# An attention and mixture-of-experts kernel: loads and TensorE order planned anew, with a charge for DMA issues that meet an instruction fetch

## The chip, the cores and the metric

One core of a Trainium2 chip runs the whole program. The metric is the device time of one execution in microseconds (us). TensorE is PE in the profile, its weight loads PEld, VectorE DVE, ScalarE ACT, GpSimd POOL, and SyncE, which issues every DMA of this kernel, SP.

## The reference, cut to what matters

```
scores = (q @ k.T) / 8                     # 8 batches, 8 heads, 576 tokens, 64 per head, float32
mask   = heads 0-3: the last 32 tokens; heads 4-7: every 32nd token
x      = softmax(scores + mask) @ v        # heads side by side: x is (8, 576, 512)
w      = softmax over the two largest of x @ w_gate, for 4 experts
out    = sum over chosen experts e:  w_e * (causal_softmax(x wq_e (x wk_e).T / 8) @ (x wv_e)) @ wo_e
```

## The kernel before, in words

The kernel is a list of 517 operations for TensorE and many more for the other engines, made batch by batch, and a planner (`schedule`, from line 584) that runs a small cost model of the chip at build time and emits every instruction in the order that it finds. At run time each engine executes its own list strictly in that order and waits on semaphores.

**Stage 1** of a batch works on four pairs of heads, called h0 to h3 here; h0 and h1 are local, h2 and h3 strided. For each pair q and k are loaded into a `nat` tile: a local pair by four issues (line 868, 144 KB each), a strided one by two loads of three issues (line 875). `tp` transposes it on PE in two halves u0 and u1 (line 921), copies bring the result to SBUF, `s` makes the scores (line 954), mask and softmax follow on DVE, POOL and ACT, and `xa` multiplies with v (line 1047 local, 1066 strided). The v of a local pair is two loads of four issues (line 898), of a strided pair one load of six (line 906). There are two buffers for `nat` and two for v (`VR`); the local pairs of batch 0 use other buffers for `nat`. So the q and k of a pair can be loaded only when `tp` of the last but one pair has ended, and its v when an earlier `xa` has ended.

**Stage 2** projects x with three-term split float32: `pj` makes q and k (line 1197; line 1208 in batch 0, there in parts of three matmuls, one for each pair of heads), `vp` and `vp4` the values and the gate (lines 1144 and 1128), `s2` and `s2_4` the causal scores (lines 1282 and 1262), `t2` transposes the probabilities (line 1336), `acc` multiplies with the values (line 1369) and `yp` with wo (line 1398); then the result is stored (lines 1407 to 1410). The weights come in at the start by line 814 (with line 817 for the gate) and are split into a high and a low half (lines 820 and 823).

**What sets the order.** `PRI` (line 109) holds a number for each operation, by kind and batch. For a PE operation the whole part is its turn: PE takes turn 0, 1, 2 and so on to 516, whatever is ready. For any other operation the number is added to a key that the program gives; among the operations of an engine that can start at the same time the planner takes the lowest key. For the loads that key, from batch 1 on, is `k0 - 30` for q and k and `k0 - 25` for v, with `k0 = 52 * (batch + 0.25 * pair)`; for batch 0 it is the pair (v: 4 + the pair), and for the weights 6.5, 7.5 and 12.5 for wk, wq and wv plus 0.1 for each slice. A load takes a free buffer when it is issued. The planner also models the fetch of PE's instructions in blocks of 256:

```
if x == ask:
    coming, ask = at + FETCH, ask + 256
else:
    end += max(here - at, 0.0)
    here, part = coming, part + 256
```

and an issue on SP as a fixed time `ask_`, a share of the DMA engines' time, and a wait for one of eight lanes (from line 674).

Of the kernel before, what the change touches and what calls it, by code (L numbers as in the profile page):

```python
# [20 lines left out]
def attention_moe_kernel(  # L21
# [59 lines left out]
    class Ring:  # L81
# [16 lines left out]
        def take(self, buf):  # L98
# [485 lines left out]
    FETCH, DMALAT = 4.2, 1.7  # L584
# [891 lines left out]
```

## Time and profile before

| | us |
|---|---|
| median of 3 runs | 464.77 (463.95 to 467.97) |
| time of the profiled execution | 465.67 |
| its span, first to last instruction | 463.9 |
| PE busy | 442.1 (95%) |
| DVE, ACT, POOL busy | 334.7, 280.3, 214.6 |

The profiled execution's time is 1.77 us more than its span, and 0.9 us above the median. The kernel's bytes are 41.94 MB of DMA at a mean of 90 GB/s. A reader should look at PE's idle time first, then at the clock that was granted while it ran, and then at which stretch of the span either falls into.

### The profile page before, as it was taken

What the parts mean: (1) busy time and instruction counts of PE and PEld (TensorE: products, weight loads), DVE (VectorE), ACT (ScalarE), POOL (GpSimd) and SP (SyncE); (2) the same over time, 40 slices, a digit from 0 to 9 for tenths busy, and PEclk for the clock granted to TensorE, in tenths of its full rate; (3) what the DMA queues carried; (4) which work ended last, traced back from release to release, by engine and by line L of the source; (5) the groups of instructions that cost most, each with busy time, mean ns of one, the idle gap of its engine ahead of it and who ended that gap; (6) DMA issues with size and microseconds to landing.
All of it is one profiled execution on the core that took longest, in us unless ns stands there. A gap on an engine that the chain in (4) does not pass through costs nothing.

```text
span 463.9 us, 19970 instructions
## 1 busy us (share of the span) xinstructions
PE 442.1 (95%) x8198; PEld 396.7 (86%) x8198; DVE 334.7 (72%) x1096; ACT 280.3 (60%) x846; POOL 214.6 (46%) x384
## 2 busy tenths in 40 slices
PE   6599897989999999999999999999999999999996
PEld 5598795879989998899988899899988998899874
DVE  3867766886766879967798874786689866746760
ACT  3356666854675659746497364766567537826552
POOL 5474277546234616823447425352446624250440
PEclk9659987999999999999999999999999999999999
DMA  8556634454144027383156601534034302200013
GB/s 138 128 138 139 156 98 105 116 139 94 30 128 107 11 65 149 108 130 83 39 137 162 106 28 53 152 79 101 27 76 152 86 1 58 68 23 4 24 69 114
DMA packets 82619, 41.94 MB, mean 90 GB/s; under 512 B 70752, under 2 KB 74208, under 8 KB 82528
## 3 DMA queue, kind: packets, MB, share of 16 engines
q1 hardware_dynamic: 82528, 40.66, 36.3%
q8 instruction: 65, 1.06, 1.0%
q14 instruction: 26, 0.21, 0.2%
HBM read 31.20 MB, written 9.44 MB: 88 GB/s over the span
## 4 chain that ended last, share of the span: by engine, by line
PE 85%; SPq 6%; DMA 4%; issue 2%; ACT 1%; DVE 1%; POOL 0%; ACTq 0%
PE bank L1197 20%; PE bank L1398 11%; PE bank L1144 10%; PE bank L1369 10%; PE bank L1282 7%; PE bank L1336 6%; PE bank L954 5%; PE bank L921 4%; PE bank L1047 3%; PE bank L1262 3%; PE bank L1066 2%; SPq L868 2%; DMA nat<-in_k_dram 2%; SPq L898 2%; PE bank L1128 2%
## 5 line engine op out<-in xcount | busy, mean ns | idle before, releaser
L1317 POOL TENSOR_SCALAR p<-p,st,wt 128x384 f32<-128x384 f32 (+3 forms) x128 | 76.5, 616 | 62.2 <-DVE st L1301 31.5
L1294 ACT ACTIVATE p<-p,st 128x256 f32<-128x256 f32 (+3 forms) x128 | 71.8, 567 | 1.5 <-DVE st L1289 1.1
L1289 DVE CUSTOM_DVE_ANT_0 p<-bank,m_cau 128x384 f32<-128x384 f32 (+3 forms) x128 | 56.5, 485 | 3.1 <-PE bank L1282 2.0
L1217 ACT CAST qk<-bank 128x288 fp32r<-128x288 f32 x64 | 25.6, 400 | 52.1 <-PE bank L1197 51.6
L1369 PE MATMUL bank<-th,vs 128*64 128x192 f32 (+4 forms) x512 | 49.8, 343 | 0.0
L1219 DVE TENSOR_TENSOR qkl<-bank,qk 128x288 fp32r<-128x288 f32 x64 | 28.5, 451 | 26.1 <-ACT qk L1217 25.9
L729 ACT COPY qkt<-bank 128x324 f32<-128x324 f32 (+2 forms) x90 | 35.0, 429 | 19.7 <-PE bank L921 19.3
L729 ACT COPY th<-bank 128x384 f32<-128x384 f32 (+2 forms) x107 | 43.0, 433 | 5.4 <-PE bank L1336 4.6
L1369 PEld LDWEIGHTS bank<-th,vs 128*64 128x64 f32 x512 | 34.2, 139 | 13.5 <-issue 6.9
L1336 PE MATMUL bank<-ident,p 64*128 64x64 f32 x800 | 39.8, 227 | 0.3 <-DVE ol L1382 0.3
L1032 DVE TENSOR_TENSOR xl<-bank,xh 128x160 fp32r<-128x160 f32 (+4 forms) x112 | 30.6, 327 | 12.9 <-ACT xh L1030 11.6
L1336 PEld LDWEIGHTS bank<-ident,p 64*128 64x128 f32 x800 | 33.5, 140 | 6.5 <-issue 2.6
L921 PE MATMUL bank<-ident,nat 54*128 54x54 f32 (+1 forms) x636 | 31.9, 236 | 7.4 <-DMA nat<-in_q_dram 2.4
L1144 PE MATMUL bank<-wh_v,xh 128*128 128x260 f32 x128 | 36.6, 286 | 0.0
L1144 PE MATMUL bank<-wh_v,xl 128*128 128x260 f32 x128 | 36.3, 283 | 0.0
L1144 PE MATMUL bank<-wl_v,xh 128*128 128x260 f32 x128 | 36.0, 281 | 0.0
L1030 ACT CAST xh<-bank 128x160 fp32r<-128x160 f32 (+4 forms) x112 | 27.0, 320 | 14.6 <-PE bank L1047 10.1
L954 PE MATMUL bank<-qkt 64*32 64x64 f32 (+1 forms) x2048 | 32.7, 233 | 3.3 <-issue 2.4
L921 PEld LDWEIGHTS bank<-ident,nat 54*128 54x128 f32 (+1 forms) x636 | 27.1, 148 | 10.1 <-DMA nat<-in_q_dram 2.6
L989 POOL TENSOR_TENSOR p1l<-p1l,st 128x640 f32<-128x640 f32 (+1 forms) x18 | 20.5, 1143 | 29.3 <-DVE st L987 23.9
L954 PEld LDWEIGHTS bank<-qkt 64*32 64x32 f32 (+1 forms) x2048 | 28.5, 122 | 6.0 <-issue 3.5
L729 ACT COPY ys<-bank 128x512 f32<-128x512 f32 x29 | 17.0, 586 | 27.4 <-PE bank L1398 24.5
(154 smaller groups left out, 1336.5 us busy)
## 6 DMA issues: line engine op xcount, KB each, us to landing
out_dram<-ys SPq DMA_DIRECT2D x32, 256.0 KB
nat<-in_q_dram SPq DMA_DIRECT2D x28, 144.0 KB
nat<-in_k_dram SPq DMA_DIRECT2D x28, 144.0 KB
nat<-in_k_dram SPq DMA_DIRECT2D x32, 99.0 KB
nat<-in_q_dram SPq DMA_DIRECT2D x32, 99.0 KB
v<-in_v_dram SPq DMA_DIRECT2D x64, 48.0 KB
v<-in_v_dram SPq DMA_DIRECT2D x48, 54.0 KB
nat<-in_k_dram SPq DMA_DIRECT2D x16, 90.0 KB
```

Source lines behind the costliest of these rows:

```text
L729: (nc.scalar.copy if e == "ACT" else nc.vector.tensor_copy)(dst, src)
L921: nc.tensor.transpose(tp[x].t[:, w_ * (g - g0):w_ * (g - g0) + w_], blk, ident[r, r])
L954: nc.tensor.matmul(o, lhs, rhs, start=True, stop=True)
L1144: nc.tensor.matmul(vp.t[:m, :NV], xx.t[:, t0:t0 + m], ww.t[:, kt, :], start=i == 0, stop=i == 11)
L1197: nc.tensor.matmul(pj.t[:, :HS], ww.t[:, kt, ep * 128:(ep + 1) * 128], xx.t[:, c], start=i == 0, stop=i == 11)
L1282: nc.tensor.matmul(sp[a].t[:, :nk], x.t[r, 0, q0:q0 + 128], y.t[r, 1, :nk], start=i == 0, stop=i == 2)
L1289: lambda e, sp=sp, p=p, a=a, nk=nk, ci=ci: nc.vector.tensor_tensor_reduce(out=p.t[:, a, :nk], in0=sp[a].t[:, :nk], in1=m_cau[:, S - nk:], ...
L1294: op("exp2", {"ACT": 0.33 + 0.00083 * nk}, k_ + 1, lambda e, p=p, a=a, ci=ci, nk=nk: nc.scalar.activation(p.t[:, a, :nk], p.t[:, a, :nk], ...
L1317: lambda e, p=p, a=a, ci=ci, t=t, nk=nk: nc.gpsimd.tensor_scalar(p.t[:, a, :nk], p.t[:, a, :nk], st.t[:, 14 + ci + a:15 + ci + a], wt.t[:, ...
L1336: nc.tensor.transpose(tp[hf].t[:, 64 * c:64 * c + 64], src, ident[r, r])
L1369: nc.tensor.matmul(acc.t[o, c0:c0 + cn], vw, th[a].t[:, s0:s0 + cn], start=j == 0, stop=j == idx[-1], skip_group_check=True)
L1398: nc.tensor.matmul(yp.t[:, :DM], xx.t[:, c0:c0 + 128], ww.t[:, ep, :], start=i == 0, stop=i == 5)
```

## The change

The planner gets one more rule: when an instruction fetch has been asked for (0.5 us after the asking point), the next DMA issue on SP that lies close to that moment takes 1.0 us longer. All numbers in `PRI` are new, 517 of them turns of PE: 120 operations keep their turn, 229 move by one or two, and the farthest moves by 40. Nothing else differs: the same instructions on the same engines, the same buffers, the same data.

```
     PRI = {
...
-        "load_qk 1": [-54.5, -39.5, -359, -18.5, -36, -5.5, -29.5, 18.5, -39, -10, 37, -25],
-        "load_qk 2": [-17.5, 30, -29.5, -12, 23, 37, -26.5, 3.5, 7.5, -32, -54, -15.5],
+        "load_qk 1": [-203.5, -40.5, -578, -55.5, -242, 12.5, -49.5, -47, -35.5, -210, 58.5, -123.5],
+        "load_qk 2": [36, -5.5, -109.5, 8.5, 18.5, -36, 18.5, -44, 9, -33.5, -69.5, 25.5],
...
-        "load_v 1": [41.5, -14.5, 55, 2, 18, 18],
-        "load_v 2": [9, 17.5, 4.5, 4, -72, 8],
+        "load_v 1": [176.5, -19, -10.5, 340.5, 12.5, 34.5],
+        "load_v 2": [94.5, 36.5, 37.5, 160.5, 52.5, 90.5],
...
-        "load_w 0": [-277.5, -154, -57.5, -48, -227, -231, -55, -99, -5, -3, -5.5, -15, 478, 491],
+        "load_w 0": [-254.5, -220, -214.5, -77.5, -282.5, -245.5, -160, -59.5, -26, -30.5, -50, -34.5, 375,
+            562],
...
-        "pj 0": [18, 23, 33, 36, 21, 30, 32, 35, 19, 25, 27, 38, 16.01, 22, 28, 34, 17, 24, 31, 37, 53, 59, 63,
-            67, 58, 60, 62, 65, 57, 61, 66, 68],
+        "pj 0": [24, 29, 35, 36, 17, 20, 26, 34, 15.01, 22, 31, 38, 19, 23, 30, 33, 16, 28, 32, 37, 55, 61, 64,
+            68, 51, 54, 60, 66, 59, 62, 65, 67],
...
-        "tp 0": [3.02, 4, 1.02, 2, 8, 7.02, 10.02, 11],
-        "tp 1": [40, 39.01, 54.02, 56, 69, 55.04, 75.04, 82],
-        "tp 2": [81.02, 85, 97, 95.02, 106.04, 107, 100.03, 105],
+        "tp 0": [4, 3.02, 2, 1.02, 8, 7.02, 10.02, 12],
+        "tp 1": [39.01, 40, 56.02, 58, 69, 57.03, 74.04, 83],
+        "tp 2": [85, 81.02, 93.02, 94, 107, 104.04, 101, 98.04],
...
-        "vp 0": [50, 49, 51, 52],
+        "vp 0": [50, 53, 49, 47.01],
...
-        "vp4 0": [47.01],
+        "vp4 0": [52],
...
-        "xa 0": [12.01, 15.01, 20.04, 29.03],
-        "xa 1": [64.03, 88.03, 101.04, 110.04],
+        "xa 0": [11.02, 14.01, 21.03, 27.03],
+        "xa 1": [63.03, 89, 109, 110.02],
...
-        "yp 0": [139, 137, 103, 134],
+        "yp 0": [132, 136, 102, 174],
...
-    FETCH, DMALAT = 4.2, 1.7
+    FETCH, DMALAT, STEAL = 4.2, 1.7, 1.0
...
+        asked = 0.0
...
-                        coming, ask = at + FETCH, ask + 256
+                        coming, ask, asked = at + FETCH, ask + 256, at + 0.5
...
                     x = max(x, lane[0]) + ask_
+                    if 0.0 < asked < x:
+                        if asked > x - ask_ - 0.8:
+                            x += STEAL
+                        asked = 0.0
                     low = max(low, x) + lo_
```

## Rows read from the trace of the kernel before

**Rows 1.** The page: busy time of PE, and its granted clock in 40 slices

```profile
PE 442.1 (95%) x8198; PEld 396.7 (86%) x8198; DVE 334.7 (72%) x1096; ACT 280.3 (60%) x846; POOL 214.6 (46%) x384
...
PEclk9659987999999999999999999999999999999999
```

**Rows 2.** Who PE waited for: us, times, longest; 0 to 104, then 100 to 460

```profile
PE bank L921 <- DMA nat<-in_q_dram: 2.4, 1, 2.4
PE bank L1047 <- DMA v<-in_v_dram: 2.3, 1, 2.3
...
PE bank L954 <- issue: 1.3, 1, 1.3
...
PE bank L954 <- issue: 1.0, 1, 1.0
```

**Rows 3.** Busy time by stretch: stretch, length, PE, PEld, DVE, ACT, POOL, PEclk, DMA

```profile
57.70:61.10 3.40, 3.40 (x29) 3.28 (x27) 0.52 (x2) 2.85 (x9) 0.75 (x1) 0.50 0.49 161
...
74.70:81.60 6.90, 6.23 (x55) 4.40 (x57) 2.77 (x7) 2.96 (x9) 4.20 (x7) 0.51 0.30 87
...
102.30:459.40 357.10, 355.62 (x6224) 321.11 (x6222) 263.13 (x875) 220.00 (x672) 158.43 (x282) 1.00 0.32 79
```

**Rows 4.** The chain of waits, 0 to 104 us: start, length, what

```profile
25.00 1.71 SPq L898
...
42.88 3.45 DMA p<-in_moe_w_gate_dram
...
63.83 1.78 PE bank L1208 x12
...
71.77 3.46 DMA nat<-in_k_dram
```

**Rows 5.** SP's issues by line: ns, min/median/max, first and last start

```profile
L898 SPq DMA_DIRECT2D v<-in_v_dram x128: 311/439/1711, 11.4 to 368.5; - x128
...
L868 SPq DMA_DIRECT2D nat<-in_k_dram x28: 595/628/1587, 36.2 to 339.3; - x28
```

**Rows 6.** The DMA queues from 25 to 26.4 us: packets, MB, share

```profile
q8 instruction: 1, 0.02, 5.8%
```

**Rows 7.** SP's timeline, 0 to 60 us: start, length, issues

```profile
32.27 2.20 SPq L906 DMA_DIRECT2D v<-in_v_dram  x6
...
43.90 2.73 SPq L898 DMA_DIRECT2D v<-in_v_dram  x4
...
48.46 3.29 SPq L906 DMA_DIRECT2D v<-in_v_dram  x6
...
52.89 0.60 SPq L868 DMA_DIRECT2D nat<-in_k_dram  x1
```

**Rows 8.** PE's timeline, 52 to 82 us: start, length, instructions, idle before

```profile
54.86 0.27 PE L921 MATMUL bank<-ident,nat 64*128 64x64 f32 x1
56.97 1.77 PE L921 MATMUL bank<-ident,nat 64*128 64x64 f32 x29 [1.84 <-DVE mx L1166]
...
65.54 0.58 PE L921 MATMUL bank<-ident,nat 54*128 54x54 f32 x12
...
71.08 0.84 PE L1336 MATMUL bank<-ident,p 64*128 64x64 f32 x20
73.80 0.24 PE L921 MATMUL bank<-ident,nat 64*128 64x64 f32 x1 [1.88 <-DVE st L1267]
75.37 1.39 PE L921 MATMUL bank<-ident,nat 64*128 64x64 f32 x21 [1.33 <-DMA nat<-in_k_dram]
```

**Rows 9.** SP's timeline, 60 to 83 us

```profile
63.81 5.84 SPq L898 DMA_DIRECT2D v<-in_v_dram  x8
69.75 1.28 SPq L868 DMA_DIRECT2D nat<-in_q_dram  x2
```

**Rows 10.** SP's waits over the whole span: us, times, longest

```profile
SPq L1410 <- ACT ys L729: 63.6, 18, 11.4
SPq L1410 <- DVE st L1301: 38.0, 2, 28.2
```

833 rows, old and new, of the table PRI are left out of this document.

## The prediction

> **What bounds the kernel now.** I read the page first: PE is busy for 442.1 of 463.9 us, so 21.8 us of idle time is all that an order can win there, beside what a low clock costs [rows 1]. The row of the granted clock says where to look: everything below nine tenths lies in the first quarter. The table by stretch confirms it. From 102.3 to 459.4 us PE is busy for 355.6 of 357.1 us at the upper level, 2.4 GHz [rows 3], and its only wait on that list is 1.0 us [rows 2]. The end, 4.5 us from 459.4 to 463.9, is a copy and a store that any order has. So the change can win in the first 102 us and lose anywhere.
>
> In the first 102 us the list of waits and PE's timeline name the losses. Before 24 us PE waits 2.4 us for q and 2.3 us for v [rows 2]. At 54.86 `tp` of batch 1 pair h1 starts, does one matmul and waits 1.84 us; at 71.92 `tp` of batch 2 pair h0 is due and waits 1.88 and 1.33 us [rows 8]. Behind each of the two, after less than a microsecond, the clock stands at 1.2 GHz, for 3.4 and 6.9 us [rows 3]. At half the clock matmuls take twice as long, so these stretches cost up to 1.7 and 3.45 us more. Two waits of 1.3 and 1.0 us "issue" are PE without instructions [rows 2].
>
> Both late `tp` wait for a load. At 73.80 the page names DVE, but the second half of the same wait names the k load that was issued at 71.77 and took 3.46 us to land [rows 4, 8]. At 56.97 it names DVE again; `tp` reads only `nat`, and the last k load of its pair was issued at 52.89 [rows 7], so by the 3.46 us it lands at about 56.4. I take the load as the cause, and keep "DVE, so nothing is won" as a bound.
>
> **Why the loads were late.** An issue of line 898 has a median of 0.44 us and a maximum of 1.71, one of line 868 0.63 and 1.59 [rows 5]. The 1.71 us one is at 25.00 [rows 4], and in that very stretch a packet of the instruction queue q8 moves [rows 6]. So an issue that meets a fetch costs about 1 us more, as the new charge says. The old planner did not know it, and its loads run behind its plan.
>
> Here a rule of the Trainium skill speaks against the change. The page "Runtime: NRT & Kernel Launch", section "Instruction fetch mechanics", says that crossing a block of 256 instructions costs one tail-bump of a queue, "mostly hidden". By it the charge is for nothing, and D below is what happens. The trace disagrees, with the 1.71 us issue and with 2.3 us in which PE had no instructions.
>
> **The change part by part.** No instruction is added or removed, so every term is a wait that goes, comes or moves. I count in the time of the profiled execution, 465.67.
>
> *Up to the values of batch 0 (turn 47).* SP issues back to back and the chain runs through it to the last slice of wv at 42.88, which lands 3.45 us later [rows 4]. By the keys the same loads stand ahead of that point as before: eight for the local pairs, the strided pairs, v, wk, wq, wv, and six loads of batch 1. Their order differs, their sum does not. Two edits cost a little: `xa` of h0 (turn 11, was 12) now waits ahead of the second half of `tp` h3, which was done during that wait; and turn 47 is `vp`, whose first matmul needs wv0, now the last slice, where `vp4` needed the last slice (wv1) second. I take +0.5 us. Bounds: -0.7 (one 144 KB load of batch 1, 0.63 us, that slips behind the v of h0) and +1.5.
>
> *Batch 1 pair h1 (turn 54, now 56).* Two things move in the same direction. PE does two more parts of `pj` first; 12 such matmuls take 1.78 us [rows 4], so two parts of three take 0.9, and PE comes at about 55.8. And by the keys the last of the four loads now has 15 issues between it and the last wv, where it had 17 (4, 3, 1, 6 and 3): k of h1 (key -12) and k of pair h2 (-162) first, then v of h0 (8), q of h2 (12.5), v of h1 (29.5) and at 47.5 the other k. The old 17 took 43.90 to 52.89 and include two that met a fetch, in the rows of 2.73 and 3.29 us [rows 7]; six issues of line 906 without one take 2.20 us [rows 7]. Four of line 898 take 1.9, so the load goes about 0.5 us earlier and lands at 55.9, 56.4 at the latest. The wait shrinks from 1.84 to 0 to 0.6. I take -1.6 (bounds +0.6, if one more issue of that length falls between, and -1.84), and all of the 1.7 us of half clock behind it (bounds 0 and -1.7). What is late next is the first half of v of h0 (key 203.5), issued right behind, for `xa` some 3.5 us later: it just fits.
>
> *Batch 2 pair h0 (turn 81 in both).* Its loads need the `nat` buffer that `tp` of batch 1 h2 frees at 66.12 [rows 8], but their first issue was at 69.75, because eight issues for v of batch 1 h1, 5.84 us with two long ones, stood ahead of them on SP [rows 9]. They stood there because the old numbers gave the second v buffer to batch 2 pair h2 (key 105 - 72 = 33, ahead of 42 and 95 for the two halves of batch 1 h1), six issues at 48.46 [rows 7]. In the new table batch 1 h1 has key 29.5 and takes that buffer, batch 2 h2 has 157.5. So behind `xa` of batch 1 h0 come only six issues of line 906, 2.2 us, or 3.3 with a fetch [rows 7]. On the old clock they end at 66.0 to 67.1, and the four loads start 2.6 to 3.6 us earlier. The last lands at 71.6 to 72.6 instead of 75.2, or 1 us later if it meets a fetch. PE is due at 71.92, with the same set of operations between the two `tp`. The wait goes from 3.21 to 0 to 1.8, middle 0.7. I take -2.5 (bounds -3.2 and, if the v still stands ahead, +1.0), and of the 3.45 us of half clock 2.4 (bounds 0 and -3.45).
>
> *PE without instructions.* 2.3 us in all. The new order has fewer dense runs of short matmuls from turn 88 to 112 (`xa` and `s` are drawn apart) but a denser one at turns 72 to 78, ahead of a wait. I take half: -1.2 (bounds -2.3 and +2.3).
>
> *The steady part.* PE's modes change 151 times instead of 149, and the same matmuls remain: 0. The old order has 1.5 us of idle time in 357 [rows 3], which is hard to repeat; I add 1.4 us for new small waits (bounds 0 and one wait like that of batch 2 h0 with its clock, 3.2 + 3.45 = 6.65).
>
> Sum: +0.5 - 1.6 - 1.7 - 2.5 - 2.4 - 1.2 + 1.4 = -7.5 us, so 465.7 - 7.5 = 458.2 for an execution like the profiled one. That one is 0.9 above the median of its runs, so the median should be 457.3.
>
> **The rivals.** *A, the waits shrink but the clock falls all the same.* A wait of 0.6 us at 54 and of 1.8 us at 72 leaves both half-clock stretches. For it: the first fall came behind a single wait of 1.84 us. Against: the 1.0 us wait between 102.3 and 459.4 brought none, the granted clock there is 1.00 [rows 2, 3]. Time: without the 4.1 us of clock and with 1.1 us less of the wait at 72, 457.3 + 5.2 = 462.5.
>
> *B, everything early goes.* Both waits, both stretches and all of "issue": 0.5 - 1.84 - 1.7 - 3.2 - 3.45 - 2.3 = -12, so 453.
>
> *C, slower: a load stuck behind a store.* SP waits in order, and it stands before the stores of line 1410 for 63.6 and 38.0 us, once for 28.2 [rows 10]. The new table moves `yp` a lot (batch 0, last full tile: turn 134 to 174), so stores sit at other places in SP's list. If a store comes late by more than the slack of the loads behind it, `tp` waits like at 73.80, 6.65 us with its clock. One such place eats most of the gain; from two on the kernel is slower: with three, 457.3 + 3 x 6.65 - 1.4 = 475.9, with two 469.2. Against it: the old order had no such case in seven batches, and the new plan charges SP more, so it leaves more room.
>
> *D, the charge decides nothing.* If the order of the first 60 us is set by free buffers and not by keys, both waits stay, and the rest balances: 464.8. For it: SP is never without a next load there, so no order makes its sum shorter. Against: what decides at 54 and 72 is which load stands where, and that does change.
>
> **How the numbers follow.** The forecast, 455 to 460, has 0.48; A 0.27; B 0.08; C 0.14; D 0.03. The predicted time is 457.3. About two in ten lie outside 453 and 465.5: most of C, and a little of B. Against the median of 464.77, 1%, about what a measurement of this kernel tells from no change, is 460.1. The forecast is below it but for its uppermost part (0.46 and 0.02), B is below; A and D are within: faster 0.54, same 0.32, slower 0.14.
>
> **What would show it.** Right: in the profile after, no wait above 0.6 us at `tp` of batch 1 h1 and below 1.8 at batch 2 h0; six issues of line 906 on SP between `xa` of batch 1 h0 and the loads of batch 2 h0, not eight of line 898; the clock at the upper level from about 34 us on, or with one dip; PE busy without a gap from 94 to 97 us on instead of 102.3, and idle for under 4 us from there to its end. Wrong: a wait for `nat` or v behind a store (C), a dip as long as before behind a shorter wait (A), or turn 47 later than 48 us, which would mean that the early loads do not sum to the same.

## The result and the profile after

The changed kernel takes 461.91 us (median of 17 runs, 458.57 to 467.35), the kernel before, run in turn with it on the same chip, 467.97 (17 runs). The ratio is 0.9916, 95% interval 0.9887 to 0.9945: 0.8% faster. Two later runs of the changed kernel beside that of before gave 0.9898 (0.9841 to 0.9956) and 0.9898 (0.9847 to 0.9949). The forecast was 457.3 (455 to 460) against 464.77, a ratio of 0.984. So the sign came out, and a good half of the size; the median lies 1.9 us above the range. Ratios leave out executions more than 1.5% above the fastest of their kernel (in the later comparisons 33 of 93 of the kernel before), and the two medians, which are of all, are 1.3% apart.

The page of the changed kernel, against [rows 1]: the profiled execution took 465.0 us with a span of 463.2, three above its median.

```profile
PE 439.4 (95%) x8198; PEld 394.9 (85%) x8198; DVE 338.7 (73%) x1104; ACT 279.0 (60%) x842; POOL 213.1 (46%) x380
...
PEclk9659999999999999999999999999999999999999
```

PE is busy 2.7 us less with the same 8198 matmuls, and the two slices below nine tenths at 60 and 75 us are gone from the row of the granted clock. From 34 us on it stands at the upper level, 2.4 GHz. "The same instructions on the same engines" (The change) does not hold: DVE has 8 instructions more, ACT and POOL 4 fewer each. The planner gives copies to ACT or DVE and some subtractions to DVE or POOL, and the new plan moves a few of them. In kernels with the charge the lines behind the planner are 5 higher (L926 is L921 of before).

I cut each execution at the starts of turn 47 (values of batch 0) and turn 113 (both tables have the same operations ahead of it; "head" and "rest" below are what lies ahead of and behind it). By stretch (stretch, length, busy times of PE, PEld, DVE, ACT and POOL, granted clock, DMA share, GB/s), first the kernel before:

```profile
46.65:102.27 55.62, 48.77 (x1159) 42.02 (x1157) 41.12 (x121) 37.88 (x113) 30.84 (x45) 0.91 0.51 123
102.27:459.34 357.07, 355.64 (x6226) 321.14 (x6222) 263.16 (x875) 220.00 (x672) 158.43 (x282) 1.00 0.32 79
```

The changed kernel, in the profile handed out with it, and then in two more executions (after_again and after_third below):

```profile
47.75:97.71 49.96, 44.37 (x1159) 39.37 (x1157) 42.52 (x126) 35.98 (x108) 29.51 (x43) 1.00 0.55 132
97.71:458.63 360.92, 356.81 (x6226) 322.01 (x6222) 263.92 (x875) 221.20 (x673) 158.72 (x282) 1.00 0.31 79
```

```profile
46.53:95.11 48.58, 44.12 (x1160) 39.17 (x1158) 43.14 (x126) 36.02 (x108) 29.53 (x43) 1.00 0.58 135
95.11:455.32 360.21, 356.95 (x6226) 321.93 (x6222) 264.08 (x875) 221.20 (x673) 158.73 (x282) 1.00 0.31 79
```

```profile
46.73:96.14 49.41, 44.45 (x1159) 39.37 (x1157) 42.33 (x126) 35.50 (x108) 29.45 (x43) 1.00 0.57 133
96.14:452.49 356.35, 355.88 (x6226) 321.69 (x6222) 263.84 (x875) 221.20 (x673) 158.05 (x282) 1.00 0.31 80
```

The stretch from turn 47 to 113 shrank from 55.62 us to 49.96, 48.58 and 49.41: 6.3 us won. PE's busy time in it fell by 4.5 us at a clock of 1.00 in place of 0.91; the rest, 1.8 us, is waits. The stretch behind it, from turn 113 to the last matmul, grew from 357.07 to 360.92, 360.21 and 356.35, by 2.1 us in the mean. Turn 47 starts 0.35 us later in the mean. The sum, -3.9 us, agrees with the ratios (0.9916 would be -3.9 us, 0.9898 -4.7), though it stands on one execution of the kernel before.

Who PE waited for between turns 47 and 113, in the profile handed out with the changed kernel (engine, line, releaser: us, times, longest):

```profile
PE bank L1071 <- issue: 1.3, 1, 1.3
PE bank L1341 <- POOL p L1322: 1.3, 1, 1.3
PE bank L926 <- issue: 0.9, 1, 0.9
PE bank L926 <- DVE st L983: 0.8, 1, 0.8
PE bank L926 <- ACT p L1299: 0.6, 1, 0.6
PE bank L1287 <- DVE qkl L1224: 0.6, 1, 0.6
```

The waits of 1.84, 1.88 and 1.33 us at the two `tp` [rows 8] are gone; at batch 2 pair h0 0.6 us is left (L926, ACT p). In their place stand five others of 0.6 to 1.3 us, two of them PE without instructions, which the old list had once, with 1.3 us [rows 2]. SP's timeline shows the loads as planned:

```profile
61.11 4.25 SPq L911 DMA_DIRECT2D v<-in_v_dram  x6
65.64 0.60 SPq L873 DMA_DIRECT2D nat<-in_q_dram  x1
66.34 2.22 SPq L873 DMA_DIRECT2D nat<-in_k_dram  x2
```

Six issues of the v load (line 906 of before) stand ahead of the loads for batch 2 pair h0, which begin at 65.64 where they began at 69.75 [rows 9].

### The profile page after: what moved, and what is told of

The parts are those of the page before. It is cut to its first block, busy times and chain, and to the rows that moved or that the text cites. A ratio compares the mean times of both kernels' runs of the same rounds, so it can differ in the third digit from the quotient of the medians.

```text
span 463.2 us, 19950 instructions
## 1 busy us (share of the span) xinstructions
PE 439.4 (95%) x8198; PEld 394.9 (85%) x8198; DVE 338.7 (73%) x1104; ACT 279.0 (60%) x842; POOL 213.1 (46%) x380
## 4 chain that ended last, share of the span: by engine, by line
PE 82%; SPq 7%; DMA 5%; issue 2%; ACT 1%; DVE 1%; POOL 0%; POOLq 0%; ACTq 0%
PE bank L1202 20%; PE bank L1403 11%; PE bank L1374 9%; PE bank L1149 9%; PE bank L1287 7%; PE bank L1341 6%; PE bank L959 5%; PE bank L926 4%; DMA nat<-in_q_dram 3%; PE bank L1052 3%; PE bank L1267 3%; PE bank L1071 2%; SPq L903 2%; SPq L873 2%; PE bank L1133 1%
## 5 line engine op out<-in xcount | busy, mean ns | idle before, releaser
L1299 ACT ACTIVATE p<-p,st 128x512 f32<-128x512 f32 (+3 forms) x128 | 71.7, 567 | 2.1 <-DVE st L1294 1.9
L1294 DVE CUSTOM_DVE_ANT_0 p<-bank,m_cau 128x512 f32<-128x512 f32 (+3 forms) x128 | 56.8, 485 | 3.0 <-PE bank L1287 1.4
L1374 PE MATMUL bank<-th,vs 128*64 128x192 f32 (+4 forms) x512 | 48.4, 337 | 1.4 <-DVE xl L1037 1.4
L734 ACT COPY th<-bank 128x256 f32<-128x256 f32 (+2 forms) x98 | 39.9, 432 | 10.3 <-PE bank L1341 9.7
L734 ACT COPY qkt<-bank 128x324 f32<-128x324 f32 (+2 forms) x83 | 32.2, 425 | 17.9 <-PE bank L926 17.7
L926 PE MATMUL bank<-ident,nat 54*128 54x54 f32 (+1 forms) x636 | 31.8, 232 | 5.6 <-DMA nat<-in_q_dram 3.3
L734 ACT COPY ys<-bank 128x512 f32<-128x512 f32 x32 | 18.8, 586 | 28.8 <-PE bank L1403 25.9
L734 DVE COPY th<-bank 128x384 f32<-128x384 f32 (+2 forms) x62 | 29.7, 489 | 8.2 <-PE bank L1341 8.0
L926 PEld LDWEIGHTS bank<-ident,nat 54*128 54x128 f32 (+1 forms) x636 | 26.7, 144 | 8.6 <-DMA nat<-in_q_dram 3.0
L1202 PE MATMUL bank<-xh,wh_q 128*128 128x288 f32 x112 | 33.6, 300 | 0.0
```

The source lines that it names most:

```text
L734: (nc.scalar.copy if e == "ACT" else nc.vector.tensor_copy)(dst, src)
L926: nc.tensor.transpose(tp[x].t[:, w_ * (g - g0):w_ * (g - g0) + w_], blk, ident[r, r])
L1202: nc.tensor.matmul(pj.t[:, :HS], ww.t[:, kt, ep * 128:(ep + 1) * 128], xx.t[:, c], start=i == 0, stop=i == 11)
L1294: lambda e, sp=sp, p=p, a=a, nk=nk, ci=ci: nc.vector.tensor_tensor_reduce(out=p.t[:, a, :nk], in0=sp[a].t[:, :nk], in1=m_cau[:, S - nk:], ...
L1299: op("exp2", {"ACT": 0.33 + 0.00083 * nk}, k_ + 1, lambda e, p=p, a=a, ci=ci, nk=nk: nc.scalar.activation(p.t[:, a, :nk], p.t[:, a, :nk], ...
L1374: nc.tensor.matmul(acc.t[o, c0:c0 + cn], vw, th[a].t[:, s0:s0 + cn], start=j == 0, stop=j == idx[-1], skip_group_check=True)
```

## The experiments

### One key, and one key with one turn

The v load of batch 2 pair h2 was named as what kept the old loads late. one_key changes that number alone; key_and_one_turn also moves the values of batch 1 pair h1 behind two neighbours; key_and_turns takes turns 76 to 89 in the new order instead. All three on the kernel before, without the charge.

```
-        "load_v 2": [9, 17.5, 4.5, 4, -72, 8],
+        "load_v 2": [9, 17.5, 4.5, 4, 52.5, 8],
```

key_and_one_turn, besides:

```
-        "acc 0": [84, 90, 98, 112],
+        "acc 0": [84, 89, 98, 112],
-        "s 1": [44.01, 72, 73, 89],
+        "s 1": [44.01, 72, 73, 88],
-        "xa 1": [64.03, 88.03, 101.04, 110.04],
+        "xa 1": [64.03, 90.03, 101.04, 110.04],
```

key_and_turns, besides (five more rows likewise):

```
-        "acc 0": [84, 90, 98, 112],
+        "acc 0": [88, 90, 98, 112],
-        "tp 2": [81.02, 85, 97, 95.02, 106.04, 107, 100.03, 105],
+        "tp 2": [85, 81.02, 97, 95.02, 106.04, 107, 100.03, 105],
-        "xa 1": [64.03, 88.03, 101.04, 110.04],
+        "xa 1": [64.03, 89, 101.04, 110.04],
```

> The kernel before with one number changed: the key of the v load of batch 2 pair h2 goes from -72 to 52.5 (no charge), so that batch 1 h1 gets the second v buffer. My theory of the second wait: its four q and k loads for batch 2 h0 start right behind the transposes of batch 1 h2, the wait at 72 us falls from 3.2 us to under 1.2 and the 6.9 us of half clock go, -5 to -6.5 us before turn 113, ratio 0.986 to 0.990. Rival: the wait is set by how late the buffer is free, it stays above 2 us, ratio 0.997 to 1.001.

> The kernel before with the one load key (-72 becomes 52.5) and one turn of TensorE moved: the values of batch 1 pair h1 go from turn 88 to 90, behind the fourth scores and the second product of batch 0; no charge. Theory J in its smallest form: the wait of 3.03 us at these values and its low clock go, turn 113 at 96 to 98.5 us, ratio 0.985 to 0.995. Rival O (the gain needs the whole plan): a wait of 2 us or more with a low clock at another place before 100 us, turn 113 at 99.5 to 102, ratio 0.996 to 1.008.

> The kernel before with one load key (the v of batch 2 pair h2: -72 becomes 52.5) and with turns 76 to 89 of TensorE in the new order (the values of batch 1 pair h1 go behind its fourth scores and one more product); no charge, the rest of the table old. Theory J (loads and turns must change together: the one key uncovers the wait of 3.03 us at the values of batch 1 pair h1, the turns hide it): no wait over 1 us and no low clock between 50 and 100 us, turn 113 at 96 to 98 us (102.3 before), ratio 0.985 to 0.995. Rival O (the gain needs the whole new plan): a wait of 2 to 3 us with a low clock turns up at another place before 100 us, turn 113 at 99.5 to 102, ratio 0.996 to 1.004.

one_key: ratio 0.998 (0.9944 to 1.0016), where 0.986 to 0.990 was expected. Both late loads were mended by the one number: `tp` of batch 1 h1 waited 0.34 us, that of batch 2 h0 not at all, and it started at 69.62 in place of 73.80. But PE then came early to the values of batch 1 pair h1, whose transposed probabilities DVE had not finished. PE's waits from 70 to 102 us:

```profile
PE bank L1047 <- DVE pt L1008: 3.0, 1, 3.0
PE bank L954 <- issue: 0.6, 1, 0.6
...
```

In the kernel before DVE had ended this transpose at 79.11, and PE came to the values at 82.08, so it had 3.0 us to spare:

```profile
78.27 0.84 DVE L1008 STREAM_TRANSPOSE pt<-p1l 128x640 f32<-128x640 f32 x1
```

With the wait of 3.0 us in one_key the clock stood at 1.2 GHz for 6.8 us (77.55 to 84.38), as it had behind the load. The stretch to turn 113, against 55.62:

```profile
46.95:99.78 52.83, 47.33 (x1160) 40.96 (x1158) 40.30 (x121) 35.98 (x108) 29.76 (x44) 0.94 0.53 122
```

key_and_one_turn: ratio 0.9966 (0.9935 to 0.9996). That wait went with the one turn, the clock stayed up, and the stretch took 51.00 us:

```profile
46.34:97.34 51.00, 46.05 (x1160) 39.52 (x1158) 41.99 (x123) 37.30 (x112) 30.73 (x45) 1.00 0.56 130
```

So four numbers out of the whole table bring 4.6 of the 6.3 us of this stretch. The rest of this execution gave 4.6 back, 361.70 against 357.07, with a wait of 2.0 us for instructions at 354 us and 6.8 us at the lower clock behind it; it is an execution 3.2 us above its median. The ratio missed the expected 0.985 to 0.995; what theory J said of the stretch itself came, turn 113 at 97.34 and no low clock before it.

key_and_turns: ratio 1.0071 (1.0027 to 1.0116). A larger edit of the same neighbours (14 turns where key_and_one_turn moves 3), and two new waits, PE from 60 to 102 us:

```profile
PE bank L1018 <- POOL p1s L989: 4.7, 1, 4.7
PE bank L954 <- issue: 2.3, 1, 2.3
...
```

The first of them is at turn 92, behind the new order. The second is at turn 72, ahead of every turn that was moved, so the order did not make it. A load that is late hides the next thing that is late. Which that is, hangs on the order of a few neighbours.

### The charge and the table, each alone

table_alone is the new table with the charge left out; charge_alone is the kernel before with the charge.

```
-                    if 0.0 < asked < x:
-                        if asked > x - ask_ - 0.8:
-                            x += STEAL
-                        asked = 0.0
```

(charge_alone adds these lines.)

> The new table with the charge left out: TensorE's order is the changed kernel's, on SP 17 of 371 places differ. Theory N (the table carries the gain, the charge nothing): ratio 0.989 to 0.995 like the change, turn 113 at 97 to 98.5 us, no low clock after 34 us in most executions. Rival K (the charge carries it): the loads run behind the plan again, a wait of 1 us or more for a load between 50 and 100 us, ratio 0.996 to 1.004.

> The kernel before with the charge alone: TensorE's order is that of before, on SP 31 of 372 places differ. Theory N: the waits at the two tp (54 and 72 us) and their low clock stay, turn 113 at 101.5 to 103, ratio 0.997 to 1.004. Rival K: the loads go earlier by the charge, turn 113 before 99 us, ratio 0.985 to 0.995.

table_alone: 1.0153 (1.0105 to 1.02), slower. charge_alone: 1.0058 (1.0018 to 1.0098), slower. Neither theory stands: the table does not carry the gain without the charge, and the charge brings none to the whole time without the table. In table_alone PE's order is that of the changed kernel and SP's differs at few places (17 of 371 by the expectation), but PE waits from 58 to 107 us for:

```profile
PE bank L1336 <- POOL p L1317: 8.8, 2, 5.3
PE bank L1208 <- ACT qkt L729: 3.6, 1, 3.6
...
```

POOL's timeline of table_alone shows where the first of these comes from (start, length, instructions):

```profile
80.22 1.28 POOL L980 TENSOR_TENSOR p1s<-p1s,st 128x648 f32<-128x648 f32 x1 [3.29 <-DVE st L978]
81.85 2.83 POOL L1317 TENSOR_SCALAR p<-p,st,wt 128x256 f32<-128x256 f32 x5 [0.35 <-DVE st L1301]
84.65 1.27 POOL L989 TENSOR_TENSOR p1s<-p1s,st 128x648 f32<-128x648 f32 x1
86.26 0.77 POOL L1317 TENSOR_SCALAR p<-p,st,wt 128x512 f32<-128x512 f32 x1 [0.34 <-DVE st L986]
```

and that of the changed kernel:

```profile
74.43 3.25 POOL L1322 TENSOR_SCALAR p<-p,st,wt 128x256 f32<-128x256 f32 x6
```

The scaling of the probabilities of batch 0 starts at 81.85 in place of 74.43 and is cut by steps of other softmaxes of 1.27 us, on which PE's next transposes hang. The planner orders DVE, ACT and POOL by its own clock: who is ready first, then the key. The charge shifts that clock, so the same keys give another order on engines that it doesn't name; the 3.6 us for ACT are of the same kind. The charge is not a gain of its own here; it is the condition under which the new numbers mean what they do. In charge_alone, waits for k stayed at the two `tp` (0.9 and 3.0 us). Yet in the profiled execution turn 113 came at 97.75, as rival K had it, and 6.15 us of waits followed, 3.5 of them for a q load at 250 us. Of what the change wins in the first stretch, the charge alone won 4.0 us in that execution, and lost 8.2 in the second:

```profile
46.10:97.75 51.65, 46.09 (x1159) 39.87 (x1157) 42.73 (x124) 36.26 (x107) 31.07 (x44) 0.97 0.48 126
97.75:462.99 365.24, 358.37 (x6226) 323.11 (x6222) 261.31 (x874) 221.12 (x673) 157.53 (x284) 1.00 0.30 78
```

That an issue on SP can be long beside a fetch is borne out. In the 16 traces together 392 of 7072 issues took over 0.5 us more than the median of the issues of the same line and tensor (0.89 us in the middle of them), and 388 of the 392 overlap a 16 KB packet of the instruction queue q8. But of all issues that overlap such a packet only a quarter were long (388 of 1640), so 1.0 us each time is a rough figure.

### Parts of the table

new_head_old_rest takes everything up to turn 112 and the loads of batches 0 to 2 from the new table, the rest from the old; old_head_new_rest the reverse, except that the v loads of batch 2 keep the new numbers, the mended key of one_key among them; old_new_loads is the old table with the new loads of batches 0 to 2; new_order_old_loads the new table with all old loads. All with the charge. Two rows of 17 in new_order_old_loads, against the changed kernel (old_new_loads is the reverse for batches 0 to 2 and the weights, 7 rows; of the two mixes one row of some 316 is shown):

```
-        "load_v 1": [176.5, -19, -10.5, 340.5, 12.5, 34.5],
-        "load_v 2": [94.5, 36.5, 37.5, 160.5, 52.5, 90.5],
+        "load_v 1": [41.5, -14.5, 55, 2, 18, 18],
+        "load_v 2": [9, 17.5, 4.5, 4, -72, 8],
```

new_head_old_rest, against the changed kernel:

```
-        "acc 4": [336, 347, 348, 386],
+        "acc 4": [334, 345, 346.02, 384],
...
```

> PE turns 0 to 112 (and the keys of what belongs to them, and all loads of batches 0 to 2) as in the changed table, everything from turn 113 on as in the old one; both tables have the same set of operations ahead of turn 113. Theory H (the change wins some 4.5 us before turn 113 and its new order loses over 3 us again after it): turn 113 at 97 to 98 us, PE idle for about 1.5 us from there on, ratio to before 0.982 to 0.987. Rival R (what is won early is lost later whatever the order, or the difference is scatter between executions): ratio 0.990 to 0.994, as the changed kernel.

> The reverse: turns 0 to 112 from the old table, the rest from the changed one. H: the two early waits and both low stretches of the clock are back, turn 113 near 102 us, and the new rest costs 3 us more than the old: ratio 1.004 to 1.010. R: 0.998 to 1.002.

> The old table, with the charge, and only the keys of the loads of batches 0 to 2 and of the weights from the changed one; PE's order is the old one. If the order of the loads alone makes the early gain: no wait above 1 us at the transposes of batch 1 h1 and batch 2 h0, no fall of the clock after 34 us, turn 113 at 96 to 99 us, ratio 0.984 to 0.992. If PE's order has to change with it: at least one of the two waits stays at 1.5 us or more with its low clock, turn 113 at 100 us or later, ratio 0.996 to 1.002.

> The changed kernel with the loads' keys of the kernel before; TensorE's order, the charge and every other key are the new ones. Theory J (loads and turns must change together): the loads at the two tp of batch 1 h1 and batch 2 h0 come late again, a wait of 1 us or more with a low clock at one of them, ratio 0.996 to 1.01. Rival T (the order of TensorE carries the gain, the loads follow free buffers): no wait over 1 us for a load between 50 and 100 us, ratio 0.988 to 0.994.

| run | ratio (95%) | turn 113 at | from there to the last matmul | the largest new waits |
|---|---|---|---|---|
| new_head_old_rest | 1.0035 (1.0 to 1.007) | 95.47 us | 361.57 us | 2.3 us for a q load at 248, 1.7 without instructions |
| old_head_new_rest | 1.0008 (0.9972 to 1.0044) | 100.41 | 356.65 | 5.5 for DVE at the values of batch 1 h1 |
| old_new_loads | 1.0049 (1.0015 to 1.0083) | not read: its profiled execution took 476.06 us, 8 above its median | | |
| new_order_old_loads | 1.0264 (1.022 to 1.0308) | 105.56 | 364.77 | 4.5 twice for a v load |

The new head works without the new rest: turn 113 came at 95.47. But the old rest, started 6.8 us earlier than in the kernel before, took 361.57 where it had taken 357.07. Most of these 4.5 us is one load. Planned with the charge, the old rest is not in its old order: on SP the q load of batch 5 pair h2, right behind its k load in the kernel before, comes after 14 issues for v and two stores. First before, then new_head_old_rest, with the wait:

```profile
238.42 1.22 SPq L875 DMA_DIRECT2D nat<-in_k_dram  x3
239.68 1.05 SPq L875 DMA_DIRECT2D nat<-in_q_dram  x3
```

```profile
233.21 1.23 SPq L880 DMA_DIRECT2D nat<-in_k_dram  x3
...
243.93 1.05 SPq L880 DMA_DIRECT2D nat<-in_q_dram  x3
```

```profile
PE bank L926 <- DMA nat<-in_q_dram: 3.1, 3, 2.3
```

PE waited 2.3 us for it at turn 286, and the clock stood at 1.2 GHz for 3.4 us. The q load at 250 us in charge_alone is the same one, in the same place on SP; key_and_one_turn, as early but planned without the charge, keeps it right behind k and has no wait there. This is rival C in small. The ratio of a whole run is the wrong place to look for a stage. The reverse keeps the old head's order of PE, and there the wait behind the mended load came again, as in one_key:

```profile
PE bank L1052 <- DVE pt L1013: 5.5, 1, 5.5
```

With the old loads under the new order PE waits for v until 99 and 134 us:

```profile
PE bank L1052 <- DMA v<-in_v_dram: 4.5, 1, 4.5
PE bank L1071 <- DMA v<-in_v_dram: 4.5, 1, 4.5
```

In none of the four did a part of the table bring what the whole brings.

The planner says as much before anything runs. Its cost model stands in each kernel.py, and the end that it reckons there for PE's last operation, with the charge, is 450.6 us for the changed kernel, 455.8 for old_head_new_rest, 458.7 for new_head_old_rest, 459.0 for old_new_loads, 459.9 for charge_alone and 469.2 for new_order_old_loads: the order of the measured ratios, of which the middle four lie within each other's intervals. (spread, below, is reckoned 453.9 and measured like the changed kernel.) Its plans hold the long waits too: 4.5 us at turn 88 in old_head_new_rest, 3.0 for the q load at turn 286, 6.9 and 7.1 for v in new_order_old_loads, and without the charge 2.9 at turn 88 in one_key, 4.7 at turn 92 in key_and_turns, and 3.2 and 5.1 in table_alone. What the plan of the kernel before did not hold is the two waits at `tp` (0.9 us at turn 81 and none at 54, where the trace has 3.2 and 1.8). So the mixes were slower by their plans already; they do not test what the chip does with an order planned as well as the whole.

### The same kernel again, and 64 instructions more

after_again and after_third are the changed kernel unaltered. shift_64 puts 16 matmuls of one column, 64 instructions, behind the warm-up; their products are not used.

```
             nc.tensor.matmul(wb.t[:, :256], ones[:, :128], ones, start=True, stop=True)
+        for _ in range(16):
+            nc.tensor.matmul(wb.t[:32, :1], ones[:, :32], ones[:, :1], start=True, stop=True)
```

> The changed kernel once more, unaltered, beside the other three. Theory W (what it gives back after turn 113 is waits that change from execution to execution, mostly TensorE without instructions): turn 113 at 97 to 98.5 us again, but the late waits are others than 1.4 us at 241.6 and 1.0 at 298.9; ratio 0.988 to 0.995. Rival P (they belong to the new order): the same turns wait again, by 0.7 to 1.3 times as long, the same ratio.

> The changed kernel with 16 matmuls of one column (64 instructions of TensorE) put behind the warm-up, where TensorE waits for the first loads; all else in the same order. Theory F (TensorE without instructions is a fetch of 256 instructions that comes late at counts that leave 193 or 194 when divided by 256, and the order is laid out around these places): the stalls move to other turns but stay at the same remainder, they sum to 10 to 25 us in place of 4.2 to 4.6, ratio to before 1.01 to 1.05. Rival M (the stalls belong to the operations, not to the count): the same turns 98, 109, 340 and 418 stall, sum 3 to 6 us, ratio 0.985 to 0.995.

> The changed kernel, unaltered, beside the version with the three products spread. Theory F: stalls without instructions of 4 us or more in the profile again, at turns 98, 109, 340 and 418; ratio to before 0.988 to 0.995, and 1 to 3 us above the spread version in the medians.

Between turns 47 and 113 the waits were, in after_again and then in after_third:

```profile
PE bank L1071 <- issue: 1.4, 1, 1.4
PE bank L1341 <- POOL p L1322: 1.3, 1, 1.3
PE bank L926 <- issue: 0.9, 1, 0.9
...
```

```profile
PE bank L1071 <- issue: 1.4, 1, 1.4
PE bank L926 <- DMA nat<-in_q_dram: 1.2, 2, 0.9
PE bank L1341 <- POOL p L1322: 1.1, 1, 1.1
PE bank L1287 <- DVE qkl L1224: 0.9, 1, 0.9
...
```

So the largest of them belong to the new order (rival P): the stall at turn 109 stands in all three executions, the wait for POOL too, the one at 98 in two. In all, PE went without instructions for 4.20, 4.63 and 1.72 us, in the kernel before for 2.40. That they would all recur, as expected of after_third, was wrong. Behind turn 113 theory W holds: the waits at turns 277, 340 and 418 were 1.4, 1.0 and 0.7 us, then 0.6, 0.9 and 1.0, and after_third had none of them.

Where they lie is told by counting PE's instructions in the trace (weight loads, matmuls and waits on semaphores) up to the stall; here are the two of the kernel before, those of the changed kernel over 0.3 us and four of shift_64's:

```
kernel         turn  ends at   stall us   instructions before it   remainder of 256
before          102    94.44    1.35         3522                   194
before          295   258.37    1.05        10178                   194
changed          98    86.11    0.94         3266                   194
changed         109    94.46    1.33         3777                   193
changed         340   298.90    1.00        11714                   194
changed         418   362.24    0.72        14273                   193
shift_64         95    85.31    2.20         3266                   194
shift_64        111    98.54    2.00         4033                   193
shift_64        176   165.60    1.71         6337                   193
shift_64        315   287.25    1.30        10945                   193
```

In the 15 profiles counted in this way (all but old_new_loads) 50 of 54 stalls over 0.3 us leave 193 or 194; the other four last 0.33 to 0.36 us. The planner holds these places already: `part` starts at 193 and grows by 256. The queue of instructions moves packets of 16 KB, 65 of them in the changed kernel, about one for each 256 of PE's 16,620 instructions. Put the n-th packet beside the n-th of these places after the first. In all 16 traces PE passed none of them sooner than 1.20 us after the end of its packet, and at each of the 61 stalls over 0.2 us that lie there it went on 1.2 to 1.75 us after that end. So such a stall is a fetch that comes too late.

shift_64 shows what the place is worth: ratio 1.0222 (1.0173 to 1.0272). Twelve stalls, 13.4 us, all at the same remainders; the turns 98, 109, 340 and 418 of the changed kernel no longer stall, others do. Its list has

```profile
PE bank L959 <- issue: 6.2, 4, 2.2
PE bank L1052 <- issue: 2.4, 2, 1.7
...
PE bank L1149 <- issue: 1.3, 1, 1.3
...
```

with four smaller lines of stalls. Not one operation was reordered. The order of PE, then, is laid out around these places, and 64 instructions more at the start break it.

The Trainium skill, page "Runtime: NRT & Kernel Launch", section "Instruction fetch mechanics", says that crossing a block of 256 instructions is "mostly hidden". The trace agrees for most: of 65 crossings in the changed kernel one to five did not hide, in shift_64 twelve, and these cost up to 2.2 us each.

### Three products spread

If the stalls are the gain that was missing, a long product ahead of a stalled turn should bring it. spread moves three turns of the changed kernel: 112 to 109, 336 to 339, and 419 to 418.

```
-        "acc 0": [88, 90, 96, 112],
+        "acc 0": [88, 90, 96, 109],
-        "acc 4": [336, 347, 348, 386],
+        "acc 4": [339, 347, 348, 386],
-        "yp 5": [428, 432, 480, 419, 443],
+        "yp 5": [428, 432, 480, 418, 443],
...
```

> The changed kernel with three long products of TensorE moved in front of turns that stalled for instructions: the last product of batch 0 (turn 112) ahead of the values at 109, the first of batch 4 (336) between the scores at 339 and 340, one output product of batch 5 (419) ahead of the scores at 418. Theory F: the three stalls of 1.3 to 1.4, 0.9 to 1.0 and 0.7 to 1.0 us go, the sum of these waits falls from 4.2 to 4.6 to under 2 us, ratio to before 0.981 to 0.988. Rival V (each moved product uncovers another wait, as the edits of the kernel before did): the time stays within 0.3% of the changed kernel, ratio 0.988 to 0.995, or gets worse.

> The version with the three products spread once more. Theory F (the stalls are the gain that was missing): under 2.5 us of them in the profile, median 1 to 3 us below the changed kernel, ratio to before 0.982 to 0.989. Rival V (what they cost is given back at other waits): within 0.7 us of the changed kernel.

spread: ratio 0.9911 (0.9878 to 0.9944). spread_again: 460.98 us beside after_third's 459.32, ratio 0.9928 (0.9894 to 0.9962). The stall at 109 is gone in both, and the stretch from 47 to 113 took 47.64 and 47.91 us, 1.5 less than in the changed kernel:

```profile
46.51:94.15 47.64, 44.55 (x1160) 39.70 (x1158) 41.85 (x126) 35.82 (x108) 29.34 (x40) 1.00 0.60 141
46.60:94.51 47.91, 44.25 (x1159) 39.28 (x1158) 42.54 (x125) 36.23 (x109) 29.24 (x40) 1.00 0.64 144
```

But without instructions PE went 2.21 and 3.43 us, in the second with a stall of 1.5 us at turn 98 and 0.75 at 340, and from turn 113 on it took as long as the changed kernel (358.61 and 360.87). So theory F falls as an account of the missing microseconds: these stalls come and go between executions of one kernel by more than the edit moves. No version here beats the changed kernel by what can be measured.

## Why the prediction was right in sign and wrong in size

By its own terms, with the mean of three profiled executions of the changed kernel against the one of before:

| term | forecast | measured |
|---|---|---|
| up to turn 47 | +0.5 | +0.35 |
| the two waits at `tp` | -1.6 and -2.5 = -4.1 | -4.7 |
| half clock behind them | -1.7 and -2.4 = -4.1 | -4.5 |
| other waits between turns 47 and 113 | 0 | +1.9 |
| PE without instructions, whole span | -1.2 | +1.1 |
| the rest behind turn 113 | +1.4 | +1.9 |
| sum | -7.5 | -3.9 |

The sum was off by 3.6 us. The step that failed is the one that put every other wait at nothing: such waits came to 1.9 us, and PE without instructions, forecast to shrink by 1.2 us, grew by 1.1. The last term, right in the mean, was luck: against the kernel before, the three executions took 3.9 and 3.1 us more behind turn 113, and 0.7 less.

**Right.** Why the loads were late, and that the six-issue load takes the place of the eight; one_key shows that with that number alone. It went a little further than said: the loads began at 65.64, not at 66.0 to 67.1, although the six issues took 4.25 us and not 2.2 to 3.3, because they began at 61.11. The clock was worth what its stretches said, and all of both came back. It is about as much as the whole gain. Of the executions behind the two later ratios the mean granted clock is 0.9705 before (24, mean 464.10 us) and 0.9783 in the changed kernel (12, mean 460.14). With two levels, full and half, the time at the lower one is twice the missing share of the span: some 27 and 20 us. If half of the difference was lost, that is an estimate of 3.7 us, where the means differ by 4.0. Rival A, waits that shrink and a clock that falls all the same, did not come: behind the 0.6 us left at batch 2 h0 the clock stayed up.

**Wrong: "what is late next".** The text asked the question at the first stall, answered it with the next load alone ("it just fits"), and did not ask it at the second. The next in line were for the most part no loads: POOL's scaling at the second product transpose (1.32, 1.31 and 1.07 us in the three), the `tp` of batch 2 h1 (0.81 for DVE, under 0.2, and 0.89 for a q load), the scores at 64 us (0.55, under 0.2 and 0.89). In the old trace PE, held up by the loads, found them done and did not wait, so no list of waits names them; how long they had been done I never read. one_key has the clearest case: 4.2 us won at turn 81, 3.0 lost at turn 88, whose input had been ready for 3.0 us in the old trace and was ready only 1.4 us earlier in the new one.

**Wrong: "PE without instructions, I take half".** The sign was guessed from how dense the runs looked. Where such stalls can lie is fixed by the count of instructions, and that could have been read in the trace of before (both its stalls have the remainder 194) or in the planner; which turns the new order puts there was not looked up. Which of the places then stall in an execution is not shown by any run. Its own bounds, -2.3 to +2.3, held the +1.1.

**D, the charge decides nothing,** was given 0.03 because the order of the loads would change. That is what came; but the text took charge and table for one thing, and they are two: alone, the charge is 0.6% slower, the table 1.5%.

**The signs it named** (no wait over 0.6 us at one `tp` and 1.8 at the other, the six issues, the clock, turn 47 ahead of 48 us) came, and still half of the gain did not. None of these looked at the stretch between. The one that did look at the end of it, PE busy from 94 to 97 us on and then idle for under 4 us, just failed in the profile handed out (97.71, and 4.1 us idle) and came in the other two.

What stays open: which stalls for instructions come in an execution and which don't, with the same instructions at the same counts (4.63 and 1.72 us in two runs of one kernel); and why the new rest loses 2.1 us in the mean. There a sum of waits that differ each time was seen, no one cause.

## What to carry to other kernels

A wait that goes is worth its length only down to the next operation that was late behind it; read for each turn after it how long its inputs had been ready, on every engine, before the wait's length goes into a sum. Where the clock falls behind a wait, the clock's part belongs to the gain (4.5 us here, with 4.7 of the waits themselves), but it is lost again behind the next wait, as in one_key. And a planned order is fitted to its planner and to the count of instructions: a piece of it, or the same order shifted by 64 instructions, can be slower than what it replaced. Where a planner has a cost model, read its plan of each version first: here it held most of the long waits that the mixes showed.

## What was not expected of the hardware

TensorE's stalls for instructions lay at fixed places in its list, at counts of 193 or 194 past a multiple of 256, as the planner has them. Not foreseen was their price: 64 instructions more at the start, which do nothing, made the changed kernel some 15 us slower (ratio to before 1.0222 in place of 0.990), 9 to 12 of them as such stalls (13.4 us against 1.7 to 4.6). The same kernel, unaltered, had 4.63 us of them in one execution and 1.72 in another. And SyncE's issues were long almost only beside an instruction fetch: 388 of the 392 that took over 0.5 us more than their median overlap a packet of that queue.
